# PSUM as eight single-bank tiles instead of two double and four single ones, in a fused linear-attention and token-mixing kernel

## The chip, the cores and the metric

The kernel runs on one core of a Trainium2 chip. The metric is device time in microseconds; smaller is better. A core has five engines that take instructions from queues of their own, each in its written order: TensorE (PE; its weight loads are shown as PEld), VectorE (DVE), ScalarE (ACT), GpSimd (POOL) and SyncE (SP), which here only issues DMA transfers. Matmuls write into PSUM, a memory of eight banks of 512 float32 values in each of 128 partitions; everything else lives in SBUF.

## The reference

```python
def _attn_ref(r, k, v, w, u):            # r, k, v: (4, 8, 768, 48)
    for t in range(S):
        cur = einsum('bhd,bhe->bhde', u[None] * kt, vt)
        y[:, :, t] = einsum('bhd,bhde->bhe', rt, state + cur)
        state = w[None, :, :, None] * state + einsum('bhd,bhe->bhde', kt, vt)

def _moe_ref(x, w_theta, w_tok_r, w_tok_i, w_ch):   # x: y as (4, 768, 384)
    theta = x @ w_theta
    zr, zi = x * cos(theta), x * sin(theta)
    y = einsum('ts,bsd->btd', w_tok_r, zr) + einsum('ts,bsd->btd', w_tok_i, zi)
    u = x + y
    return u + maximum(u @ w_ch, 0.0)
```

A recurrent attention with a per-channel decay `w` and a bonus `u` for the current token gives `x`. Two 768 x 768 matrices then mix the tokens of `x`, rotated by an angle that depends on `x` itself, and a last matrix mixes the channels.

## The kernel before, in words

The tokens of each of the four batches are cut into six chunks of 128, and chunks are taken in pairs: a step `g = 3 * b + pr` is one pair, twelve in all. The recurrence becomes matmuls in chunk form: decayed copies of r and k, scores within a chunk under a triangular mask, and a state handed from chunk to chunk.

`attention(b, pr, base)` makes the tasks of one step. POOL (in the first steps DVE) scales r and k by powers of the decay (`rscale`, L553; `kscale`, L566 and L569), PE transposes them through PSUM (`flips`, L516), and ACT or DVE copies them out (L275, L277). In the first batch (`pj`) the loads hold two neighbouring tokens in one row, and PE puts v back into order (`V`, L600), with a copy `Vev` behind it (L604). `scores` (L614) makes, for each chunk, eight 64-row matmuls, one for each head; even and odd heads go to the two banks of a double tile. `mask` (L619) multiplies the 1024 results by the mask into `mAT`. `PD`, `diag` and `dg` work out the bonus term, and POOL spreads it over v (`yd`, L648). `outer` (L672, L680) and `S` (L690, L700) carry the state. `y` (L712, L717) is one piece for each chunk, both in one double tile; then `x` (L726) adds `yd` for both chunks at once. `x` is transposed, in steps 0 to 5 on PE, from step 6 on by a DMA transpose issued by SP (`turn`, L529). `theta` (L743) multiplies it by `w_theta` for both chunks in one piece, ACT takes the sine (L747) and, in place, the cosine (L750), DVE makes `zr` (L753), POOL `zi` (L756).

`mixing(b, pr, base)` makes, for each chunk of the output, six pieces `mix` of two matmuls (L774), each over one pair of chunks of `zr` or `zi`. They add up in a single bank. `un` (L782) adds x. `un` is transposed (on PE in steps 0 to 3 and 11, otherwise by DMA), `f` (L799) multiplies it by `w_ch` for two chunks, `fin` (L804) is ReLU plus `un`, and SP stores the result (L808). Only the last step does this part chunk by chunk. `token_weights` casts and transposes the two mixing matrices, twelve blocks (`Wcast`, `Wflip` L500, `Wevac`).

The order is written out. `Plan.add` collects each task with its engines, its keys read and written, and the PSUM tiles that it takes (`acq`, with the number of banks) or uses. `ORDER` is a list of (task number, engine, tile numbers ...); `Plan.follow` walks it and emits the tasks in that order, so that each engine's queue has the list's order, and every PSUM tile is the one that the list names. PSUM is cut by

```python
SLOTS = (2, 2, 1, 1, 1, 1)
banks = [ps.tile([C, n, 512], F32, name=f"bank{i}") for i, n in enumerate(SLOTS)]
```

Tasks of two banks (`dbl`: y, theta, f, scores, V) can only take tiles 0 and 1; tasks of one bank may take any. Semaphores between tasks follow from the reads and writes of tiles.

Among the tasks are 108 of the name `warm` (L817), each of two 128 x 128 matmuls on zeros. They compute nothing that is used. The list puts them where PE is to be kept going.

The costs written in the tasks (`dve_op`, `act_op`, `pe_op`, the pairs of SP's loads) were for the search that made the list; when the kernel is built, only the list decides.

Of the kernel before, what the change touches and what calls it, by code (L numbers as in the profile page):

```python
# [22 lines left out]
SLOTS = (2, 2, 1, 1, 1, 1)  # L23
# [4 lines left out]
    (0, 2), (4, 1), (10, 3), (3, 1), (2, 1), (16, 0, 0), (1, 2), (144, 4), (14, 3), (11, 1), (17,  # L28
    0, 3), (7, 2), (13, 3), (145, 4), (32, 0, 4), (8, 3), (33, 0), (18, 2), (34, 0), (12, 3), (9,
    1), (146, 4), (35, 0), (6, 1), (21, 2), (36, 0), (37, 0), (23, 2), (38, 0), (15, 3), (5, 1),  # L30
    (39, 0), (40, 0), (19, 2), (41, 0), (42, 0), (24, 2), (179, 4), (43, 0), (44, 0), (22, 2),
    (45, 0), (150, 1), (46, 0), (47, 0), (20, 2), (48, 0), (49, 0), (50, 0), (153, 2), (51, 0),
    (147, 1), (178, 4), (151, 0, 3), (52, 0), (53, 0), (25, 0, 2), (152, 2), (148, 0, 1), (26, 1),
    (184, 1), (54, 0), (55, 0), (212, 4), (27, 2), (56, 0), (149, 2), (57, 0), (58, 0), (164, 0,
    3), (30, 1), (59, 0), (60, 0), (61, 0), (28, 2), (62, 0), (165, 2), (160, 1), (63, 0), (31,
    3), (158, 0, 1), (140, 4), (154, 0, 0), (181, 1), (64, 0), (65, 0), (155, 2), (161, 0, 2),
    (66, 0), (67, 0), (180, 4), (159, 1), (68, 0), (69, 0), (162, 2), (182, 0, 5), (163, 3), (156,
    0, 0), (183, 2), (70, 0), (71, 0), (157, 1), (185, 0, 2), (213, 4), (72, 0), (73, 0), (74, 0),
    (186, 2), (75, 0), (76, 0), (77, 0), (215, 1), (166, 0), (78, 0), (187, 2), (168, 0, 0), (142,
    4), (79, 0), (194, 1), (169, 0), (216, 0, 2), (141, 2), (170, 1), (268, 4), (80, 0), (195, 0,  # L40
    5), (81, 0), (217, 2), (82, 0), (218, 3), (192, 0, 1), (167, 1), (188, 0, 0), (193, 1), (83,
    0), (196, 2), (270, 4), (84, 0), (189, 2), (198, 0, 5), (143, 2), (171, 0, 3), (197, 3), (190,
    0, 1), (269, 4), (29, 2), (172, 1), (85, 0), (86, 0), (87, 0), (199, 1), (173, 0, 0), (191,
    1), (214, 4), (273, 3), (219, 0, 3), (174, 2), (88, 0), (202, 0, 1), (175, 2), (89, 0), (244,
    4), (90, 0), (203, 0), (276, 3), (91, 0), (92, 0), (220, 2), (200, 0), (204, 1), (252, 4),
    (93, 0), (274, 0, 2), (221, 2), (176, 1), (205, 0, 3), (177, 3), (94, 0), (248, 4), (95, 0),
    (224, 0, 1), (206, 2), (201, 1), (222, 0, 0), (225, 1), (96, 0), (275, 2), (264, 4), (277, 0,
    5), (245, 3), (232, 0, 3), (223, 2), (278, 1), (97, 0), (260, 4), (98, 0), (253, 3), (99, 0),
    (246, 0, 2), (249, 2), (284, 1), (226, 0, 0), (207, 0, 1), (256, 4), (247, 2), (227, 1), (265,
    3), (233, 2), (100, 0), (272, 4), (250, 0, 2), (228, 1), (208, 2), (101, 0), (102, 0), (282,  # L50
    0, 0), (251, 1), (261, 3), (254, 0, 5), (209, 2), (306, 4), (283, 1), (103, 0), (104, 0),
    (229, 0, 2), (266, 0, 3), (230, 2), (255, 2), (105, 0), (262, 0, 2), (231, 3), (271, 4), (210,
    1), (106, 0), (280, 0, 0), (263, 2), (285, 0, 5), (281, 1), (234, 0, 1), (302, 4), (286, 2),
    (267, 2), (307, 3), (107, 0), (235, 0), (415, 0, 2), (257, 2), (211, 3), (236, 1), (330, 4),
    (308, 0, 5), (416, 0), (279, 2), (258, 0, 0), (309, 1), (237, 0, 3), (259, 2), (417, 0), (287,
    3), (331, 4), (238, 1), (288, 0, 1), (403, 0, 5), (289, 2), (418, 0), (404, 0), (314, 4),
    (290, 0), (335, 3), (239, 0, 0), (291, 1), (332, 4), (292, 0, 1), (293, 0), (240, 2), (396, 0,
    3), (303, 3), (294, 1), (322, 4), (405, 0), (241, 2), (406, 0), (243, 3), (397, 0), (242, 1),
    (336, 0, 1), (318, 4), (398, 0), (337, 2), (399, 0), (304, 0, 0), (310, 4), (338, 3), (407,
    0), (305, 2), (400, 0), (401, 0), (364, 4), (419, 0), (402, 1), (295, 0, 1), (323, 3), (408,  # L60
    0), (296, 1), (339, 0, 3), (311, 2), (409, 1), (365, 4), (315, 3), (420, 0), (324, 0, 0),
    (340, 1), (312, 0, 5), (319, 3), (325, 2), (421, 1), (297, 0, 1), (334, 4), (346, 1), (313,
    2), (369, 3), (342, 0, 0), (298, 2), (333, 4), (422, 0, 3), (343, 1), (347, 0, 5), (299, 2),
    (423, 0), (320, 0, 2), (328, 4), (424, 0), (348, 1), (321, 2), (300, 1), (425, 0), (366, 4),
    (410, 0, 0), (316, 0, 5), (341, 3), (411, 2), (344, 0, 1), (317, 1), (426, 0), (454, 4), (329,
    2), (345, 1), (349, 3), (350, 0, 5), (354, 0, 0), (351, 2), (455, 4), (427, 0), (434, 0, 2),
    (372, 3), (352, 0), (370, 0, 1), (353, 1), (326, 4), (355, 0), (371, 2), (428, 1), (441, 0,
    5), (356, 1), (442, 0), (367, 4), (443, 0), (301, 3), (373, 0, 1), (357, 0, 3), (374, 1),
    (486, 4), (435, 0), (358, 2), (436, 0), (380, 1), (461, 3), (378, 0, 0), (327, 2), (444, 0),
    (379, 1), (359, 0, 1), (368, 4), (381, 0, 3), (376, 0, 0), (360, 2), (456, 4), (437, 0), (491,  # L70
    3), (377, 1), (382, 2), (438, 0), (361, 2), (108, 0), (439, 0), (457, 4), (429, 0, 3), (375,
    2), (362, 1), (445, 0), (412, 0, 0), (430, 2), (453, 4), (383, 3), (492, 0, 3), (413, 1),
    (446, 0), (493, 2), (464, 3), (431, 0, 1), (488, 4), (440, 1), (447, 1), (384, 0, 2), (432,
    1), (487, 4), (448, 0, 3), (458, 3), (385, 2), (386, 0, 0), (473, 0, 5), (449, 1), (387, 0),
    (414, 4), (474, 2), (462, 0, 1), (388, 1), (569, 0, 3), (490, 4), (459, 0, 2), (494, 3), (475,
    0), (450, 0, 0), (460, 2), (476, 1), (489, 4), (463, 1), (389, 0, 5), (469, 1), (570, 0),
    (363, 3), (390, 2), (571, 0), (521, 4), (451, 1), (495, 0, 2), (391, 0, 1), (496, 1), (519,
    4), (497, 3), (502, 1), (467, 0, 0), (392, 2), (550, 0, 5), (468, 1), (551, 0), (393, 2),
    (520, 4), (552, 0), (395, 3), (506, 0, 2), (572, 0), (394, 1), (507, 2), (465, 0, 0), (607,
    4), (553, 0), (524, 3), (466, 1), (508, 0), (573, 0), (470, 0, 1), (523, 4), (554, 0), (471,  # L80
    2), (574, 0), (509, 1), (500, 0, 1), (575, 1), (527, 3), (498, 0, 0), (609, 4), (557, 0, 2),
    (501, 1), (558, 0), (525, 0, 3), (522, 4), (559, 0), (499, 1), (472, 3), (503, 0, 1), (555,
    0), (504, 2), (526, 2), (560, 0), (606, 4), (477, 0, 1), (556, 1), (478, 0), (505, 3), (561,
    0), (479, 1), (638, 4), (510, 0, 0), (530, 2), (528, 0, 3), (511, 0), (529, 2), (576, 0, 5),
    (512, 1), (539, 0, 1), (480, 4), (562, 0), (540, 2), (577, 0), (535, 1), (578, 0), (533, 0,
    0), (563, 1), (605, 4), (531, 0, 1), (579, 0), (532, 1), (536, 0, 2), (580, 0), (587, 0, 3),
    (588, 0), (513, 4), (537, 1), (534, 1), (538, 3), (589, 0), (481, 0, 1), (581, 0), (433, 4),
    (613, 3), (482, 2), (541, 0, 0), (582, 1), (542, 0), (483, 2), (640, 4), (594, 0, 2), (543,
    1), (564, 0, 5), (590, 0), (610, 3), (565, 2), (595, 0), (484, 1), (608, 4), (514, 0, 0),
    (544, 4), (566, 0, 1), (515, 2), (485, 3), (516, 2), (596, 0), (567, 1), (614, 0, 5), (671,  # L90
    4), (616, 2), (597, 0), (518, 3), (517, 1), (591, 0), (598, 0), (615, 2), (611, 0, 1), (583,
    4), (599, 0), (612, 2), (643, 3), (592, 0), (545, 0, 0), (593, 1), (600, 1), (639, 4), (619,
    0, 1), (621, 1), (546, 2), (702, 0, 2), (676, 3), (703, 0), (620, 1), (547, 2), (709, 0, 5),
    (452, 4), (622, 0, 3), (704, 0), (623, 2), (548, 1), (710, 0), (601, 4), (549, 3), (705, 0),
    (644, 0, 3), (625, 0, 1), (711, 0), (645, 2), (626, 1), (584, 0, 0), (641, 4), (646, 3), (677,
    0, 3), (568, 4), (627, 0), (712, 0), (678, 2), (628, 1), (706, 0), (624, 3), (713, 0), (585,
    1), (673, 4), (617, 0, 1), (647, 0, 3), (618, 1), (707, 0), (642, 4), (648, 2), (714, 0),
    (602, 0, 0), (708, 1), (672, 4), (654, 1), (652, 0, 1), (603, 1), (727, 0, 2), (728, 0), (674,
# [115 lines left out]
def pe_op(ns):  # L214
    return (ns, 217)
# [27 lines left out]
def build(ctx, tc, nc, r, k, v, w, u, moe_w_theta, moe_w_tok_r, moe_w_tok_i, moe_w_ch, out):  # L243
# [226 lines left out]
    def L2(i):  # L470
        return [("L", i, 0), ("L", i, 1)]
# [397 lines left out]
```

## Time and profile before

| | us |
|---|---|
| median of 6 runs | 141.61 |
| lowest to highest of them | 140.99 to 141.88 |
| the profiled execution, own time | 142.43 |
| its span, first to last instruction | 140.7 |

The granted TensorE clock of the profiled execution is 1.000. The profile shows one execution. "Busy" is the time in which an engine has an instruction under way; a matmul's length holds its fill and drain too, so that the distance from start to start of neighbours (the pitch, below) is shorter than its length. Below, the costliest groups with their counts and mean lengths, from the list of groups by line:

| group | count | mean ns |
|---|---|---|
| PE mix (L774), 128 x 384 | 288 | 326 |
| PE warm (L817), 128 x 128 | 216 | 239 |
| PE scores (L614), 64 rows | 192 | 218 |
| DVE mask (L619), 1024 elements | 24 | 1216 |
| DVE x (L726), 768 elements | 12 | 956 |
| DVE zr (L753), 768 elements | 12 | 950 |
| DVE fin (L804), 768 elements | 11 | 953 |
| DVE un (L782), 384 elements | 24 | 551 |
| ACT sin (L747), 768 elements | 12 | 811 |
| ACT cos (L750), 768 elements | 12 | 876 |
| POOL zi (L756), 768 elements | 12 | 1642 |
| POOL yd (L648), 768 elements | 12 | 1475 |

The mean DMA rate is 196 GB/s; the DMA engines are busy 90% or more of almost every fortieth of the span up to about 65 us, and less so after that.

### The profile page before, as it was taken

To read this page: it belongs to the slowest core of one execution; us is meant where nothing else is said; L and a number is where in the kernel's file an instruction comes from. 1 tells how busy PE (TensorE), PEld (TensorE's weight loads), DVE (VectorE), ACT (ScalarE), POOL (GpSimd) and SP (SyncE) were. 2 spreads that over 40 slices of the span, in tenths; PEclk is the share of its full clock that TensorE was granted. 3 is DMA by queue.
4 is the path that set the end of the run, shared out by engine and by line. 5 is a ranking of instruction groups with operands and counts; after the bars stand their busy time and mean duration, and the time that the engine had idled before them with its cause. 6 is when DMAs were issued, how large, how long until landed. Compare 5 with 4: busy or idle time off the path is not lost.

```text
span 140.7 us, 4021 instructions
## 1 busy us (share of the span) xinstructions
PE 135.7 (96%) x1670; PEld 97.6 (69%) x1670; DVE 100.5 (71%) x144; ACT 76.4 (54%) x119; POOL 85.4 (61%) x78
## 2 busy tenths in 40 slices
PE   6999999999999999999999999999999989999991
PEld 3997878778677676677568676676676645655691
DVE  1379986999457878798998876777989675344720
ACT  3786998999575965855515447855351243300200
POOL 7404379949999999299599099997264044400000
DMA  4999989999999999959997596997969296026660
GB/s 104 270 261 297 276 183 312 387 294 242 301 314 192 181 264 178 206 132 174 226 182 157 106 299 126 230 247 172 168 171 173 56 116 168 0 58 168 224 216 13
DMA packets 72444, 27.59 MB, mean 196 GB/s; under 512 B 67049, under 2 KB 70890, under 8 KB 72426
## 3 DMA queue, kind: packets, MB, share of 16 engines
q1 hardware_dynamic: 72400, 27.34, 85.2%
q8 instruction: 13, 0.21, 0.7%
q14 instruction: 5, 0.04, 0.1%
q10 hardware_dynamic: 26, 0.00, 0.0%
HBM read 20.06 MB, written 4.72 MB: 176 GB/s over the span
## 4 chain that ended last, share of the span: by engine, by line
PE 94%; DVE 2%; issue 1%; ACT 0%; DVEq 0%
PE bank L774 33%; PE bank L516 11%; PE bank L817 11%; PE bank L799 9%; PE bank L743 7%; PE bank L614 5%; PE bank L717 4%; PE bank L672 3%; PE bank L500 3%; PE bank L712 3%; PE bank L641 2%; PE bank L405 1%; PE bank L680 1%; PE bank L402 1%; DVE un L782 1%
## 5 line engine op out<-in xcount | busy, mean ns | idle before, releaser
L774 PE MATMUL bank<-zr,WrT 128*128 128x384 bf16 x144 | 33.4, 326 | 0.0
L774 PE MATMUL bank<-zi,WiT 128*128 128x384 bf16 x144 | 33.1, 326 | 0.0
L619 DVE TENSOR_TENSOR mAT<-bank,mask 128x1024 bf16<-128x1024 f32 x24 | 28.9, 1216 | 1.7 <-PE bank L614 1.6
L756 POOL TENSOR_TENSOR zi<-x,sin 128x768 bf16<-128x768 bf16 x12 | 19.7, 1642 | 10.1 <-ACT sin L747 10.1
L648 POOL TENSOR_TENSOR yd<-dg,vb 128x768 bf16<-128x768 f32 x12 | 17.7, 1475 | 12.9 <-ACT dg L275 5.3
L747 ACT ACTIVATE sin<-bank 128x768 bf16<-128x768 f32 x12 | 9.7, 811 | 19.5 <-PE bank L743 15.8
L817 PE MATMUL bank<-zeros 128*128 128x128 bf16 x216 | 19.3, 239 | 0.0
L569 POOL TENSOR_TENSOR Kw<-ld,wpinv 128x768 bf16<-128x768 f32 x9 | 16.4, 1818 | 3.3 <-DMA ld<-in_k_dram 3.3
L804 DVE SCALAR_TENSOR_TENSOR fin<-bank,un 128x768 f32<-128x768 f32 (+1 forms) x13 | 11.5, 892 | 8.6 <-PE bank L799 8.6
L774 PEld LDWEIGHTS <-WiT 128*128 128x128 bf16 x144 | 12.8, 97 | 6.8
L817 PEld LDWEIGHTS <-zeros 128*128 128x128 bf16 x216 | 15.0, 108 | 2.9 <-issue 2.0
L782 DVE TENSOR_TENSOR un<-bank,x 128x384 bf16<-128x384 f32 x24 | 12.9, 551 | 5.5 <-PE bank L774 5.3
L774 PEld LDWEIGHTS <-WrT 128*128 128x128 bf16 x144 | 12.1, 97 | 6.3
L553 POOL TENSOR_TENSOR Rw<-ld,wpow 128x768 bf16<-128x768 f32 x9 | 16.3, 1819 | 0.0
L275 ACT ACTIVATE RT<-bank 128x1024 bf16<-128x1024 bf16 x12 | 12.3, 1022 | 6.7 <-PE bank L516 6.6
L799 PE MATMUL bank<-Wch,uT 128*128 128x384 bf16 x72 | 13.7, 326 | 0.7 <-DVE un L782 0.6
L726 DVE TENSOR_TENSOR x<-bank,yd 128x768 bf16<-128x768 f32 x12 | 11.5, 956 | 3.9 <-PE bank L717 3.7
L743 PE MATMUL bank<-Wth,xT 128*128 128x384 bf16 x72 | 13.7, 326 | 0.0
L753 DVE TENSOR_TENSOR zr<-bank,x 128x768 bf16<-128x768 f32 x12 | 11.4, 950 | 2.1 <-ACT bank L750 2.1
L799 PEld LDWEIGHTS <-uT 128*128 128x128 bf16 x72 | 6.8, 98 | 5.6 <-DMA uT<-un 0.9
L750 ACT ACTIVATE bank<-bank,pi 128x768 f32<-128x768 f32 x12 | 10.5, 876 | 0.0
L275 ACT ACTIVATE uT<-bank 128x768 bf16<-128x768 bf16 (+1 forms) x5 | 3.3, 684 | 12.1 <-PE bank L516 12.0
(95 smaller groups left out, 221.3 us busy)
## 6 DMA issues: line engine op xcount, KB each, us to landing
ld<-in_r_dram SPq DMA_DIRECT2D x12, 384.0 KB, 5.5
out_dram<-fin SPq DMA_DIRECT2D x11, 384.0 KB, 2.8
ld<-in_k_dram SPq DMA_DIRECT2D x18, 192.0 KB, 5.1
ld<-in_v_dram SPq DMA_DIRECT2D x18, 192.0 KB, 5.3
ld<-in_moe_w_tok_r_dram SPq DMA_DIRECT2D x6, 384.0 KB, 5.2
ld<-in_moe_w_tok_i_dram SPq DMA_DIRECT2D x6, 384.0 KB, 5.7
ld<-in_k_dram SPq DMA_DIRECT2D x3, 384.0 KB, 6.1
ld<-in_v_dram SPq DMA_DIRECT2D x3, 384.0 KB, 5.7
```

Source lines behind the costliest of these rows:

```text
L275: nc.scalar.activation(dst, src, Act.Copy)
L516: nc.tensor.matmul(bank16(tok)[:, i * C:(i + 1) * C], s, ident, is_transpose=True, start=(i == 0), stop=(i == n - 1))
L553: P.add(mul(g, 2.15), lambda e: eng_of[e].tensor_mul(Rw[:, :, :, :D].transpose([0, 2, 1, 3]), Ls[ir].rearrange("p (h n d) -> p h n d", h=H ...
L569: eng_of[e].tensor_mul(Kw[:, :, :, :D].rearrange("p a h d -> p (a h) d"), Ls[ik].rearrange("p (a d) -> p a d", d=D), wpinv.rearrange("p a ...
L619: P.add({DVE: dve_op(8 * C)}, lambda e, tk=tk, c=c: nc.vector.tensor_mul(mAT[:, c].rearrange("p a h t -> p (a h) t"), dbl(tk).rearrange("p ...
L648: P.add({POOL: pool_op(2 * HD, 1.7)}, lambda e: eng_of[e].tensor_mul(yd.rearrange("p a (h d) -> p (a h) d", h=H), wide(dg, D), vb.rearrang ...
L743: nc.tensor.matmul(dbl(th)[:, t, :HD], xT[:, ND * t + dk, :], Wth[:, dk, :], start=(dk == 0), stop=(dk == ND - 1))
L756: P.add({POOL: pool_op(2 * HD, 1.9)}, lambda e: eng_of[e].tensor_mul(zi[:, 2 * pr:2 * pr + 2], x[:, 2 * pr:2 * pr + 2], sn), rd=xk + [("si ...
L774: nc.tensor.matmul(bank(tm)[:, :HD], WT[:, so, to * C:(to + 1) * C], z[:, so], start=(so == 0 and part == 0), stop=(part == 2 * NP - 1 and ...
L782: P.add({DVE: dve_op(HD)}, lambda e, tm=tm, t=t, to=to: nc.vector.tensor_add(un[:, t], bank(tm)[:, :HD], x[:, to]), use=[tm], rd=[("x", zj ...
L799: nc.tensor.matmul(dbl(tf)[:, t - lo, :HD], uT[:, ND * t + dk, :], Wch[:, dk, :], start=(dk == 0), stop=(dk == ND - 1))
L817: nc.tensor.matmul(bank("warm")[:, :C], zeros, zeros, start=True, stop=True, skip_group_check=True)
```

## The change

PSUM becomes eight tiles of one bank. The tasks that held a double tile take single ones: scores and V take two tiles at once, one for each half of the heads and for each chunk; y, theta and f become two tasks, one for each chunk, with one tile each. What reads them is halved with them: two masks of 512 elements for one of 1024, two x, zr, fin, sin, cos and V copies of 384 elements for one of 768. The keys by which tasks wait are cut likewise: y of a chunk waits for its own two masks, un of a chunk for its own x; the transposes, yd and zi still wait for both chunks. `ORDER` is another list, from a new search: all tasks stand in another order, and with other tiles; some copies are on another engine. Three of the costs for the search are changed (in `load` and `turn`), which has no effect on the built program but through the list. There are still 108 warm tasks.

The diff, with the order list and repetitions cut:

```diff
-SLOTS = (2, 2, 1, 1, 1, 1)
+SLOTS = (1, 1, 1, 1, 1, 1, 1, 1)
 ORDER = [
-    (0, 2), (4, 1), (10, 3), (3, 1), (2, 1), (16, 0, 0), (1, 2), (144, 4), (14, 3), (11, 1), (17,
...
+    (0, 2), (4, 1), (13, 3), (2, 1), (3, 1), (16, 0, 7), (1, 2), (146, 4), (14, 3), (17, 0, 5),
...
-        P.add({SP: (ns, 1400)}, lambda e: nc.sync.dma_start(out=dst, in_=src), wr=wr,
+        P.add({SP: (ns, 1700 if nload[0] < 8 else 2300)}, lambda e: nc.sync.dma_start(out=dst, in_=src), wr=wr,
...
-                        nc.tensor.matmul(dbl(tv)[:, c, :HD], spread[q, n, :], vj4[q, :, n, :],
+                        nc.tensor.matmul(bank(tv[c])[:, :HD], spread[q, n, :], vj4[q, :, n, :],
...
-            P.add({ACT: act_op(2 * HD), DVE: dve_op(2 * HD)}, lambda e: copy(
-                e, vb, dbl(tv)[:, :, :HD]), use=[tv], wr=[kv_], prio=pb + 1, name="Vev")
+            for c in range(2):
+                P.add({ACT: act_op(HD), DVE: dve_op(HD)}, lambda e, c=c: copy(
+                    e, vb[:, c], bank(tv[c])[:, :HD]), use=[tv[c]], wr=[kv_ + (c,)],
+                    prio=pb + 1, name="Vev")
...
-            tk = ("A", g, c)
+            tk = [("A", g, c, hi) for hi in range(2)]
...
-                        nc.tensor.matmul(dbl(tk)[:, hi, hp * C:(hp + 1) * C],
+                        nc.tensor.matmul(bank(tk[hi])[:, hp * C:(hp + 1) * C],
...
-            P.add({DVE: dve_op(8 * C)}, lambda e, tk=tk, c=c: nc.vector.tensor_mul(
-                mAT[:, c].rearrange("p a h t -> p (a h) t"),
-                dbl(tk).rearrange("p a (h t) -> p (a h) t", h=HP), bc(mask01, 1, 2 * HP)),
-                use=[tk], rd=["mask"], wr=[kM + (c,)], prio=pb + 3, name="mask")
+            for hi in range(2):
+                P.add({DVE: dve_op(4 * C)}, lambda e, tk=tk[hi], c=c, hi=hi: nc.vector.tensor_mul(
+                    mAT[:, c, hi], bank(tk).rearrange("p (h t) -> p h t", h=HP),
+                    bc(mask01, 1, HP)),
+                    use=[tk[hi]], rd=["mask"], wr=[kM + (c, hi)], prio=pb + 3, name="mask")
...
-        P.add({DVE: dve_op(2 * HD)}, lambda e: nc.vector.tensor_add(
-            x[:, 2 * pr:2 * pr + 2], dbl(ty)[:, :, :HD], yd),
-            use=[ty], rd=[ky], wr=xk, prio=pb + 5, name="x")
+            P.add({DVE: dve_op(HD)}, lambda e, c=c, ty=ty: nc.vector.tensor_add(
+                x[:, 2 * pr + c], bank(ty)[:, :HD], yd[:, c]),
+                use=[ty], rd=[ky], wr=[("x", zj, pr, c)], prio=pb + 5, name="x")
...
-            for t in range(2):
+        for c in range(2):
+            th = ("th", g, c)
+
+            def theta(e, c=c, th=th):
                 for dk in range(ND):
-                    nc.tensor.matmul(dbl(th)[:, t, :HD], xT[:, ND * t + dk, :], Wth[:, dk, :],
+                    nc.tensor.matmul(bank(th)[:, :HD], xT[:, ND * c + dk, :], Wth[:, dk, :],
                                      start=(dk == 0), stop=(dk == ND - 1))
...
-        P.add({DVE: dve_op(2 * HD)}, lambda e: nc.vector.tensor_mul(
-            zr[:, 2 * pr:2 * pr + 2], dbl(th)[:, :, :HD], x[:, 2 * pr:2 * pr + 2]), use=[th],
-            rd=xk, wr=[("zr", zj, pr)], prio=pb + 8, name="zr")
+            P.add({DVE: dve_op(HD)}, lambda e, c=c, th=th: nc.vector.tensor_mul(
+                zr[:, 2 * pr + c], bank(th)[:, :HD], x[:, 2 * pr + c]), use=[th],
+                rd=xk, wr=[("zr", zj, pr, c)], prio=pb + 8, name="zr")
...
-                        nc.tensor.matmul(dbl(tf)[:, t - lo, :HD], uT[:, ND * t + dk, :],
+                        nc.tensor.matmul(bank(tf)[:, :HD], uT[:, ND * t + dk, :],
                                          Wch[:, dk, :], start=(dk == 0), stop=(dk == ND - 1))
...
+                P.add({DVE: dve_op(HD)}, lambda e, t=t, tf=tf: nc.vector.scalar_tensor_tensor(
+                    fin[:, t], bank(tf)[:, :HD], 0.0, un[:, t], op0=Alu.max, op1=Alu.add),
+                    use=[tf], rd=[("un", g % 2, t)], wr=[("fin", g % 2, t)], prio=pb - 98,
+                    name="fin")
```

## The prediction

> **What bounds the kernel now.** First the page: busy time by engine, and the shares of the chain that ended last.
>
> ```profile
> PE 135.7 (96%) x1670; PEld 97.6 (69%) x1670; DVE 100.5 (71%) x144; ACT 76.4 (54%) x119; POOL 85.4 (61%) x78
> ...
> PE 94%; DVE 2%; issue 1%; ACT 0%; DVEq 0%
> ```
>
> TensorE is the bound: 94% of the chain lies on it. But not all of it is work. L817 is filler, matmuls on zeros that the order puts where it expects PE to have nothing to do. Two rows of PE's timeline show it at both ends (start us, length, line, count):
>
> ```profile
> 3.76 4.45 PE L817 MATMUL bank<-zeros 128*128 128x128 bf16 x40
> ...
> 134.36 3.40 PE L817 MATMUL bank<-zeros 128*128 128x128 bf16 x58
> ```
>
> The first 40 stand in 4.3 us (107 ns each), the last 58 in 3.2 us (56 ns each): PE starts at half pace, and a pair costs 0.11 us later on. The last real matmul ends at 134.36. Behind it come fin and the output, 6.4 us, as in any order. So the time is the sum of PE's real pieces, plus filler that stands among them, plus PE's waits. I added the pieces of the before order at the pitch (start to start) that the trace gives each kind: 131.6 us to the end of the real work. The trace has 134.36, so 2.75 us is waiting. Of it 2.1 us can be named, from gaps between PE's starts: 0.71 at 115, 0.36 at 133, 0.30 at 38, 0.30 at 13, 0.24 at 9, 0.15 at 33.
>
> **Two dear things on PE that are neither work nor wait.** In the PE timeline I look at what a scores piece (L614, eight matmuls on 64 of the 128 rows) costs its neighbours:
>
> ```profile
> 71.97 0.49 PE L774 MATMUL bank<-zi,WiT 128*128 128x384 bf16 x2
> 72.39 0.62 PE L614 MATMUL bank<-RT,KT 64*128 64x128 bf16 x16
> 72.94 0.50 PE L774 MATMUL bank<-zr,WrT 128*128 128x384 bf16 x2
> ...
> 96.00 0.81 PE L774 MATMUL bank<-zr,WrT 128*128 128x384 bf16 x4
> 96.74 0.40 PE L614 MATMUL bank<-RT,KT 64*128 64x128 bf16 x8
> 97.07 0.62 PE L516 MATMUL bank<-ident,Kw 128*128 128x128 bf16 x8
> ```
>
> Four L774 take 0.65 elsewhere, here 0.74: entry costs 0.09. Eight L614 then take 0.33, sixteen in a row 0.55. One scores piece inside a run takes 0.23, so leaving costs another 0.10. Each separate excursion to 64 rows costs 0.19 us. The Trainium skill says it too (TensorEngine Tiling, "Key Properties": changing the tiling mode drains TensorE), without a price; the rows give the price.
>
> **The change on PE.** The matmuls are the same 1670 in both programs. I compared the two instruction lists, which hold no times.
> - Scores and V pieces (27, all on 64 rows) stand next to another of them at 6 places before, at 11 after (nine pairs of scores, against three). Five fewer excursions: 5 x 0.19 = -0.95 us. Two one-bank tiles can be had in any two free banks, where scores needed one of two double tiles.
> - Filler pairs ahead of the last real matmul: 79 before, 76 after. 3 x 0.112 = -0.34 us. Filler at the end (29 pairs, now 32) lies under the output.
> - y, theta and f come as two pieces each, with their own waits. PE's pieces of mix also change operands and waits every two matmuls, and hold 0.325 per two (2 x 0.163): a wait that is over costs 0. Upper end, 36 more pieces at 0.03 = 1 us; I take 0, as that row is the same case.
>
> Sum on PE: -1.29 us.
>
> **The waits.** The 0.71 us at 115 shows a queue. The rows are PE's, then SP's:
>
> ```profile
> 114.19 1.14 PE L743 MATMUL bank<-Wth,xT 128*128 128x384 bf16 x6
> 115.88 1.15 PE L799 MATMUL bank<-Wch,uT 128*128 128x384 bf16 x6 [0.55 <-DVE un L782]
> ...
> 104.46 6.89 SPq L529 DMA_TRANSPOSE xT<-x  x2
> 111.46 1.23 SPq L529 DMA_TRANSPOSE uT<-un  x1
> 112.85 2.15 SPq L529 DMA_TRANSPOSE xT<-x  x1
> ```
>
> The view names un, but f(7) needs no new un: its uT transpose stood in SP behind an xT that waited for the x of step 10, was issued at 111.46 instead of about 106, and landed shortly before 115.88. In the new SP list uT(7) follows xT(10), whose x is due at about 102, and f(7) stands 6.9 us behind its last mix; a transpose took 2.8 us from issue to landing (5.5 at worst). The stall goes. The shortest distances between producer and the PE piece that reads a transposed tile are 4.1 to 4.5 us after and 4.6 to 5.3 before, so others have become tighter. I count the waits as equal: 2.75 us in both. From -1.5 (most named ones go) to +3 (below) is what I cannot exclude.
>
> **The other engines.** DVE gets 59 more instructions: 24 masks, 12 x, 12 zr, 11 fin, in halves. Rows of its timeline:
>
> ```profile
> 61.10 1.02 DVE L782 TENSOR_TENSOR un<-bank,x 128x384 bf16<-128x384 f32 x2
> 62.04 0.95 DVE L804 SCALAR_TENSOR_TENSOR fin<-bank,un 128x768 f32<-128x768 f32 x1
> 62.91 0.55 DVE L277 COPY uT<-bank 128x768 bf16<-128x768 bf16 x1
> ...
> 72.97 2.34 DVE L619 TENSOR_TENSOR mAT<-bank,mask 128x1024 bf16<-128x1024 f32 x2
> 75.23 0.55 DVE L782 TENSOR_TENSOR un<-bank,x 128x384 bf16<-128x384 f32 x1
> ```
>
> Two of 384 elements take 0.94, one of 768 takes 0.87: a split costs 0.07. A mask has a pitch of 1.13; its half of 512 elements is in no row, and lies between 0.47 (384) and 0.87 (768). On the line between them it is 0.61, so a split mask costs 0.09. Sum 24 x 0.09 + 35 x 0.07 = 4.6 us. The order also moves some evacuations between DVE and ACT; with them DVE's work at pitch goes from 95.2 to 101.7 us.
>
> Here a rule speaks against the change. The Trainium skill (VectorE: DVE Perf Modes, "The TRN2 errata") has a tensor_tensor take (N+151)/0.96 ns, a fixed 157 ns each, and says to amortize the fixed part over large tiles. By the rule 59 splits cost 9.3 us of DVE, twice the 4.6. The durations agree (2 x 0.55 against 0.956, 0.15 more), but on a busy DVE the next instruction starts 0.08 before the last has ended, and only pitch counts there. I take the row. Whether any of it reaches PE depends on the stage. I laid DVE's pitches against the 10 us stretch of PE's order that releases each: before, the fullest are 60 to 70 (9.6 of 10) and 70 to 80 (8.4). After, 40 to 50 (9.95) and 80 to 90 (9.0). All still fit, so I take 0. By the rule the six splits of 40 to 50 would cost 0.075 more each, 10.4 us in 10: DVE would run over by 0.4, and the gain would be 0.9.
>
> ACT gets 27 more (12 sin, 12 cos, 3 V), each 0.07 (as DVE) to 0.17 (uT: 0.49 for 384 elements, against 0.81): 2 to 4.6 us on an engine 54% busy, 0 on the path. If sin and cos did not hide, zr and zi would be late; the first half now starts half a theta (0.49 us) sooner, which pays for it. POOL loses four casts of 0.8 to ACT and gets three v casts from it.
>
> **Start and loads.** The first loads are now v, k, r for r, k, v; each 384 KB lands 1.5 us after the one before (landing records at 4.6, 6.1, 7.7). V goes first on PE, behind 10 filler pairs instead of 20. Its cast is on POOL (0.82) behind the v load: 5.4, in time for V at 5.9. In the before trace the first k multiply on DVE waited 1.33 us for ACT's wpinvj; in the new ACT order both wpinvj stand one place earlier. I count only the filler, 0 beyond it.
>
> **Sum.** Its own time of the profiled execution is 142.43 (span 140.7), 0.8 over the median of the six runs, 141.61. 142.43 - 1.29 = 141.1 by its account; for the median, **140.3**.
>
> **Rivals.**
> 1. Forecast, the PE sum with equal waits: 140.3, with waits that differ by 0.9 either way 139.4 to 141.2. Chance 0.46.
> 2. The freer banks also remove waits: of the 2.1 us named, those at 115, 38, 13 and 33 (1.46) go and nothing replaces them. 141.61 - 1.29 - 1.46 = 138.9. For it: the room for uT(7). Against: tighter transposes. Chance 0.14.
> 3. The gain goes into small new stalls: PE, a queue in a fixed order, loses 0.02 at each of the 59 more handoffs from DVE, 1.2 us in all: 141.5. Chance 0.14.
> 4. DVE becomes the bound from 40 to 100 us. Its work there at pitch is 47.6 before and 52.2 after, of 60. Before, the busy time by stretches leaves it 12 of these 60 us idle. If that idling is forced by order and handoffs, and only a part can be squeezed out, PE loses what is above 60: with 7.8 left nothing, with 9.1 all of the 1.29. With 10 left it loses 2.2, and the time is 142.5. For it: DVE at 9.95 in one stretch, more instructions in fixed order. Against: in 60 to 70 the old order ran DVE at 9.6 with PE never short. Chance 0.26.
>
> That it does not do what it says is out: the banks and pieces are in the program.
>
> A measurement tells 0.3% (0.42 us) from no change. Faster: 1 and 2, 0.60; the same: 3, 0.14; slower: 4, 0.26. Range 138.8 to 142.7, which takes in most of 4; the forecast's own is 139.4 to 141.2.
>
> **What would show it.** L614 in nine rows of x16, end of PE's real work at 133.0 or so, 6.4 us ahead of the end; masks x48 near 0.69 us; DVE near 106 busy. I am wrong if gaps between PE's starts add up to over 4 us, above all ahead of y and mix where DVE's mask or zr is the last releaser, or if the first 35 us, full of loads, let PE wait.

## The result and the profile after

The changed kernel takes 140.16 us (median of 19 runs, 139.16 to 141.03), beside 141.42 us for the kernel before (38 runs, 140.77 to 141.98, on the same chips). The ratio is 0.991, with a 95% interval of 0.9892 to 0.9928: 1.26 us faster, which was the forecast (140.3). Ratios here and below compare means and leave out the runs of a kernel that lie over 1.5% above its fastest.

The page of the kernel after: busy time by engine, the chain that ended last, and the groups of the halved instructions (count | busy us, mean ns | idle before).

```profile
PE 133.1 (96%) x1670; PEld 96.3 (70%) x1670; DVE 107.6 (78%) x208; ACT 77.2 (56%) x142; POOL 84.9 (61%) x77
...
PE 81%; DMA 10%; DVE 6%; issue 1%; SPq 0%; ACT 0%; DVEq 0%; ACTq 0%
...
L637 DVE TENSOR_TENSOR mAT<-bank,mask 128x512 bf16<-128x512 f32 x48 | 30.9, 681 | 3.8 <-PE bank L631 3.4
...
L767 ACT ACTIVATE bank<-bank,pi 128x384 f32<-128x384 f32 x24 | 13.2, 566 | 0.0
```

DVE has 7.1 us more busy time (100.5 before) and is not the bound. PE is busy 2.6 us less (135.7 before); how much of that is time is worked out below. The chain has less of PE, since it follows three DMA transfers (a first load of k, 4.9 us, an xT and a uT, 4.5 and 4.3 us) and pieces of DVE that the chain of before does not have.

PE's timeline after, at those places (start us, length, line, count, and in brackets the idle time and the releaser that the view names; transposes are L530, scores L631, theta L760, mix L791, f L817, filler L834):

```profile
3.77 2.31 PE L834 MATMUL bank<-zeros 128*128 128x128 bf16 x20
...
11.52 0.61 PE L530 MATMUL bank<-ident,Rw 128*128 128x128 bf16 x8 [0.47 <-DVE Rw L567]
...
19.52 0.61 PE L530 MATMUL bank<-ident,Kw 128*128 128x128 bf16 x8 [0.82 <-DVE x L742]
...
117.18 0.66 PE L817 MATMUL bank<-Wch,uT 128*128 128x384 bf16 x3 [0.63 <-DMA uT<-un]
...
131.51 1.14 PE L817 MATMUL bank<-Wch,uT 128*128 128x384 bf16 x6
132.48 3.74 PE L834 MATMUL bank<-zeros 128*128 128x128 bf16 x64
```

The last real matmul ends at 132.48, against 134.36 before. Added up at the trace's pitches, as the prediction did, PE's order is 129.86 us (131.60 before) and its waits are 2.62 us (2.75 before). So in these two executions the time came out of PE's order and the waits stayed the same in sum; but they are other waits. The four largest are 0.54 at 11, 0.88 at 19, 0.26 at 85, 0.80 at 116 (from start to start; the brackets count from modelled ends and show less). Behind the one at 19 stands a scaling of k on DVE that took 2.54 us (the two other such scalings took 0.94 and 0.96). PE was ready at 18.64. This transpose reads that scaled k, which was done at 18.99; it takes tile 6, which held y of step 0, and the x that reads this y came behind the scaling and was done at 19.47. So somewhat less than half of the wait is for k itself, and the rest for the bank.

The two profiled executions are not alike. After's own time is 140.20, its median; before's was 142.43, 1.0 above its median. Their difference, 2.23, is 1.74 in the order, 0.13 in the waits and 0.37 behind the last real matmul (6.00 against 6.37). The order was to give 1.29; the 0.45 beyond that fits the start, where PE ran at half pace (a filler matmul each 107 ns, later each 56) until about 7.5 us after and 9.2 us before. In the kernel with ACT's halves below, whose start is in the old order, the half pace ended at 7.3 us and PE came to its first outer piece 0.63 us sooner than before. The page's row of the granted clock shows 9 tenths in these slices, so it does not show this slow start. Start and end vary between executions: over the profiles below the half pace ends at 6.7 to 9.2 us, and from the last real matmul to the end it is 4.3 to 6.4 us.

### The profile page after: what moved, and what is told of

It is laid out like the page before. It is cut to its first block, busy times and chain, and to the rows that moved or that the text cites. A ratio compares the mean times of both kernels' runs of the same rounds, so it can differ in the third digit from the quotient of the medians.

```text
span 138.5 us, 4123 instructions
## 1 busy us (share of the span) xinstructions
PE 133.1 (96%) x1670; PEld 96.3 (70%) x1670; DVE 107.6 (78%) x208; ACT 77.2 (56%) x142; POOL 84.9 (61%) x77
## 4 chain that ended last, share of the span: by engine, by line
PE 81%; DMA 10%; DVE 6%; issue 1%; SPq 0%; ACT 0%; DVEq 0%; ACTq 0%
PE bank L791 30%; PE bank L530 10%; PE bank L760 8%; PE bank L817 8%; PE bank L834 7%; PE bank L631 4%; DMA ld<-in_k_dram 4%; PE bank L735 3%; DMA xT<-x 3%; DMA uT<-un 3%; PE bank L514 3%; PE bank L690 3%; PE bank L730 2%; DVE Rw L567 2%; PE bank L659 2%; DVE mAT L637 1%
## 5 line engine op out<-in xcount | busy, mean ns | idle before, releaser
L637 DVE TENSOR_TENSOR mAT<-bank,mask 128x512 bf16<-128x512 f32 x48 | 30.9, 681 | 3.8 <-PE bank L631 3.4
L791 PE MATMUL bank<-zi,WiT 128*128 128x384 bf16 x144 | 33.7, 326 | 0.0
L791 PE MATMUL bank<-zr,WrT 128*128 128x384 bf16 x144 | 33.2, 326 | 0.0
L764 ACT ACTIVATE sin<-bank 128x384 bf16<-128x384 f32 x24 | 11.8, 496 | 14.8 <-PE bank L760 11.9
L567 POOL TENSOR_TENSOR Rw<-ld,wpow 128x768 bf16<-128x768 f32 x10 | 18.2, 1816 | 0.0
L834 PE MATMUL bank<-zeros 128*128 128x128 bf16 x216 | 18.0, 230 | 0.0
L791 PEld LDWEIGHTS <-WiT 128*128 128x128 bf16 x144 | 12.8, 97 | 6.9
L791 PEld LDWEIGHTS <-WrT 128*128 128x128 bf16 x144 | 12.7, 97 | 6.9
L770 DVE TENSOR_TENSOR zr<-bank,x 128x384 bf16<-128x384 f32 x24 | 12.9, 550 | 5.0 <-ACT bank L767 5.0
L821 DVE SCALAR_TENSOR_TENSOR fin<-bank,un 128x384 f32<-128x384 f32 x24 | 12.9, 551 | 4.2 <-PE bank L817 4.1
L834 PEld LDWEIGHTS <-zeros 128*128 128x128 bf16 x216 | 14.1, 103 | 3.0 <-issue 2.0
L817 PE MATMUL bank<-Wch,uT 128*128 128x384 bf16 x72 | 14.8, 326 | 0.6 <-DMA uT<-un 0.6
L760 PE MATMUL bank<-Wth,xT 128*128 128x384 bf16 x72 | 15.3, 326 | 0.1
L742 DVE TENSOR_TENSOR x<-bank,yd 128x384 bf16<-128x384 f32 x24 | 12.9, 551 | 0.8 <-PE bank L735 0.6
L767 ACT ACTIVATE bank<-bank,pi 128x384 f32<-128x384 f32 x24 | 13.2, 566 | 0.0
L289 ACT ACTIVATE Sb<-bank 64x192 bf16<-64x192 f32 x20 | 6.5, 324 | 8.3 <-PE bank L690 8.1
L817 PEld LDWEIGHTS <-uT 128*128 128x128 bf16 x72 | 6.6, 98 | 4.7 <-DMA uT<-un 1.0
```

The lines of the kernel that those rows point to most:

```text
L289: nc.scalar.activation(dst, src, Act.Copy)
L567: P.add(mul(g, 2.15), lambda e: eng_of[e].tensor_mul(Rw[:, :, :, :D].transpose([0, 2, 1, 3]), Ls[ir].rearrange("p (h n d) -> p h n d", h=H ...
L637: P.add({DVE: dve_op(4 * C)}, lambda e, tk=tk[hi], c=c, hi=hi: nc.vector.tensor_mul(mAT[:, c, hi], bank(tk).rearrange("p (h t) -> p h t", ...
L760: nc.tensor.matmul(bank(th)[:, :HD], xT[:, ND * c + dk, :], Wth[:, dk, :], start=(dk == 0), stop=(dk == ND - 1))
L767: P.add({ACT: act_op(HD, True, True)}, lambda e, th=th: nc.scalar.activation(bank(th)[:, :HD], bank(th)[:, :HD], Act.Sin, bias=pi2), use=[th],
L791: nc.tensor.matmul(bank(tm)[:, :HD], WT[:, so, to * C:(to + 1) * C], z[:, so], start=(so == 0 and part == 0), stop=(part == 2 * NP - 1 and ...
```

## The experiments

Each kernel was timed beside the kernel before; ratios are to it.

### Excursions to 64 rows

In the order after, eight pairs of scores pieces were parted by one PE piece, so that there are eight more excursions (the first of eight such moves):

```diff
-    (307, 0, 4, 5), (314, 0, 1), (337, 4),
+    (314, 0, 1), (307, 0, 4, 5), (337, 4),
```

> The new kernel, in which the second scores piece of each of the eight late pairs is put behind the PE piece that followed the pair, so that eight more excursions to 64 rows are made; nothing else moves. PE sum: 8 x 0.19 = 1.5 us more than the new kernel, 141.7, that is the time of before and a little over. If excursions do not matter for the time and the gain came from tiles and order otherwise: within 0.4 us of the new 140.2. If the later second mask matters too: more than 2 us.

Measured: 141.24 us (140.59 to 142.54, 12 runs), ratio 1.0012 [0.9981, 1.0043]. Against after's 0.991 that is 1.0%, 1.4 us with some 0.5 either way, or 0.18 for each excursion. In the trace the same matmuls take 0.21 us longer at each of the eight places, 1.70 in all. One of them, after:

```profile
74.58 0.62 PE L631 MATMUL bank<-RT,KT 64*128 64x128 bf16 x16
75.13 0.50 PE L791 MATMUL bank<-zi,WiT 128*128 128x384 bf16 x2
75.47 0.49 PE L791 MATMUL bank<-zr,WrT 128*128 128x384 bf16 x2
```

and with the pair parted (one line lower in that kernel):

```profile
75.45 0.40 PE L632 MATMUL bank<-RT,KT 64*128 64x128 bf16 x8
75.78 0.50 PE L792 MATMUL bank<-zi,WiT 128*128 128x384 bf16 x2
76.21 0.40 PE L632 MATMUL bank<-RT,KT 64*128 64x128 bf16 x8
76.54 0.50 PE L792 MATMUL bank<-zr,WrT 128*128 128x384 bf16 x2
```

From the first score to the second mix is 0.89 in the one, 1.09 in the other: the same 18 matmuls cost 0.20 more. The five excursions that the change saves are worth 0.9 us by the times and 1.06 by the traces.

### Halves without the new tiles and order

The kernel before, with its double tiles and its order, but mask, x, zr, fin, sin, cos and the V copy each issued as two instructions:

```diff
-        P.add({ACT: act_op(2 * HD)}, lambda e: nc.scalar.activation(
-            sn, dbl(th)[:, :, :HD], Act.Sin), ...
+        P.add({ACT: act_op(2 * HD)}, lambda e: [nc.scalar.activation(
+            sn[:, a], dbl(th)[:, a, :HD], Act.Sin) for a in range(2)], ...
```

> The old order and the old double tiles, but mask, x, zr, fin, sin, cos and the V copy each as two instructions of half the size, one right behind the other, 59 more on DVE and 27 more on ACT. If the halving hides (PE sum): DVE busy rises by some 7 us, PE's real work ends within 0.4 us of the old 134.4, and the time is that of before within 0.3% (141.2 to 141.8). If DVE limits (rival 4): DVE was short of time at 60 to 80 and 100 to 110, so 1 us or more is lost, 142.4 or more, with gaps on PE ahead of y and f.

Measured: 144.36 us (143.58 to 145.08), ratio 1.0201 [1.017, 1.0233]: +2.9 us. Halves alone cost; that they cost nothing needs the rest of the change. So they were taken apart: the same edit on DVE's instructions only, and on ACT's only.

> The old order with the halves on DVE alone (mask, x, zr, fin; 59 more instructions); sin, cos and the V copy whole. Halving all cost 2.9 us. If DVE's load is what the old order could not bear: most of it, 143.5 or above. If the chain through ACT (theta, sin, cos, zr, then the tile is free) was: little, 141.4 to 142.2.

> The old order with the halves on ACT alone (sin, cos, V copy; 27 more instructions); DVE as before. If ACT's chain is the cause of the 2.9 us: 143 or above, since two halves of a cos took 1.14 us where the whole took 0.88, and zr, which sets the tile free for the next PE piece, comes that much later. If DVE's load is: 141.4 to 141.9.

DVE only: 141.13 us (12 runs), ratio 0.9975 [0.9955, 0.9995]: no cost in time. In its trace PE came to theta(10) 0.67 us later than before (114.86 against 114.19) and caught up at f(7), whose transpose landed in 2.8 us there and in 4.4 before (below), so small costs along the way are not excluded. ACT only: 143.40 us (143.33 to 143.68), ratio 1.0137 [1.0112, 1.0163]: +1.9 us. The chain by engine says the same; DVE only, then ACT only:

```profile
PE 95%; DVE 2%; DMA 1%; ACT 0%; issue 0%
```

```profile
PE 68%; ACT 16%; DVE 5%; issue 3%; DMA 3%; POOL 2%; POOLq 0%; ACTq 0%; DVEq 0%
```

The ACT timeline of one step shows what a split costs. Before:

```profile
46.57 0.82 ACT L747 ACTIVATE sin<-bank 128x768 bf16<-128x768 f32 x1
47.26 0.90 ACT L750 ACTIVATE bank<-bank,pi 128x768 f32<-128x768 f32 x1
48.10 0.81 ACT L275 ACTIVATE WrT<-bank 128x768 bf16<-128x768 bf16 x1
```

ACT halved, the same step:

```profile
46.61 0.88 ACT L747 ACTIVATE sin<-bank 128x384 bf16<-128x384 f32 x2
47.52 1.14 ACT L750 ACTIVATE bank<-bank,pi 128x384 f32<-128x384 f32 x2
48.59 0.80 ACT L275 ACTIVATE WrT<-bank 128x768 bf16<-128x768 bf16 x1
```

From the sine to what stands behind the cosine it is 1.53 us before and 1.98 in halves: 0.45 a step, 0.22 a split. In the trace the halves do not overlap here: each cosine half waits for a semaphore that ACT itself sets at its instruction before. In the kernel after, where each half has a tile of its own, they overlap by some 0.1 us:

```profile
49.11 0.48 ACT L764 ACTIVATE sin<-bank 128x384 bf16<-128x384 f32 x1
49.48 1.03 ACT L767 ACTIVATE bank<-bank,pi 128x384 f32<-128x384 f32 x2
50.41 0.83 ACT L289 ACTIVATE WrT<-bank 128x768 bf16<-128x768 bf16 x1
```

The second sine takes 0.37 us and the two cosines 0.93 from start to start, so that two of each are some 1.67 us, against 1.53 whole: 0.07 a split. That the tiles make the difference fits these waits; no run has tiles of its own with the old order. In the old order zr waits for both cosines, and PE's next scores wait for the double tile that zr frees. PE's timeline of the ACT-halved kernel:

```profile
49.71 0.40 PE L614 MATMUL bank<-RT,KT 64*128 64x128 bf16 x8 [0.28 <-DVE zr L753]
```

Like this one (0.35 from start to start), two more waits at 72 and 123 us have zr behind them, 0.25 and 0.42; one of 0.47 at 61 has a copy of uT on ACT. They are most of the 1.9. After the change no wait of PE above 0.2 us has zr or a cosine behind it. DVE's and ACT's halves together cost 1.3 us more than their sum (2.9 against 1.9 and -0.35). In the profiles 1.07 of this stands ahead of f(7), where PE waited 0.87 us in the kernel with all halves, 0.49 with ACT's, 0.02 with DVE's and 0.71 before; there the landing of one transpose decides (below), so it need not be a cost of the splits.

### Smaller pieces still

After, with each mask as two of 256 elements: 48 more DVE instructions.

```diff
-                    mAT[:, c, hi], bank(tk).rearrange("p (h t) -> p h t", h=HP), bc(mask01, 1, HP)),
+                    mAT[:, c, hi, q:q + 2], bank(tk).rearrange(...)[:, q:q + 2],
+                    bc(mask01, 1, 2)) for q in (0, 2)],
```

> The new kernel with each mask as two instructions of 256 elements, 48 more on DVE at about 0.08 us each by the rows of the halved kinds, 3.9 us of DVE work. If DVE still hides: within 0.4 us of the new 140.2. If the new order has used up DVE's room (40 to 50 us was 9.95 of 10): 1 us or more, 141.2 or above, with gaps on PE ahead of y.

Measured: 141.13 us (139.58 to 141.93, 12 runs), ratio 0.9956 [0.9923, 0.9988]; against after 0.46%, +0.65 us with an interval of about 0.5 either way, for 48 more splits (DVE's busy time grows by 2.7 us, to 110.3). DVE is close to the bound only in one stretch. The busy times from 20 to 30 us (PE, PEld, DVE, ACT, POOL; clock, DMA share, GB/s), after:

```profile
20.00:30.00 10.00, 10.00 (x187) 8.45 (x185) 10.00 (x20) 9.38 (x18) 7.01 (x6) 1.00 0.91 248
```

with quarters:

```profile
20.00:30.00 10.00, 9.71 (x175) 8.09 (x175) 10.00 (x27) 8.27 (x18) 6.40 (x5) 1.00 0.93 260
```

There DVE is full in both, and with quarters PE no longer is.

### The wait at 115 in the order before

The prediction put the 0.71 us before f(7) down to SP's order. Test: in the order before, SP issues uT(7) ahead of xT(10).

```diff
-    (665, 4), (694, 0), ..., (747, 0), (734, 4),
+    (694, 0), ..., (747, 0), (734, 4), (665, 4),
```

> The kernel before with SP's transpose uT of step 7 put ahead of xT of step 10, so that it is issued when its un is done (about 110.6) instead of at 111.46. If the 0.71 us wait of PE at 115 came from SP's order, as the prediction had it: it goes, 140.7. If un itself, late on DVE behind three masks, set it: the transpose is issued at 110.6 at the earliest and 0.0 to 0.5 us is saved, 140.9 to 141.4.

Measured: 142.46 us (9 runs), ratio 1.0069 [1.0039, 1.0099]: 1.0 us slower. SP's timeline in that kernel:

```profile
104.37 2.03 SPq L530 DMA_TRANSPOSE xT<-x  x1
110.54 1.21 SPq L530 DMA_TRANSPOSE uT<-un  x1
111.81 3.26 SPq L530 DMA_TRANSPOSE xT<-x  x2
```

uT(7) still could not be issued before 110.5, and xT(10) now stood behind it; theta(10) on PE then waited 1.47 us for it (3.9 us from its issue to its landing). One cause is one engine further back, in DVE's timeline of before:

```profile
105.66 3.48 DVE L619 TENSOR_TENSOR mAT<-bank,mask 128x1024 bf16<-128x1024 f32 x3
109.16 0.96 DVE L726 TENSOR_TENSOR x<-bank,yd 128x768 bf16<-128x768 f32 x1
110.03 0.55 DVE L782 TENSOR_TENSOR un<-bank,x 128x384 bf16<-128x384 f32 x1
```

The un that uT(7) transposes stood behind three masks and an x, though its last mix had ended at 106.6. So the next run moved this un ahead of one mask and the x, and uT(7) ahead of xT(10) as before:

```diff
-    (684, 1), ..., (693, 0, 0), (726, 1), (665, 4), ..., (734, 4),
+    (726, 1), (684, 1), ..., (693, 0, 0), (734, 4), (665, 4), ...,
```

> The kernel before with the un of step 7 (mix of chunk 2, batch 2) put one mask and one x earlier in DVE's order, and the DMA transpose uT of step 7 ahead of xT of step 10 on SP. If DVE's order was the cause of PE's wait at 115 (un done at 110.5 in before), un is done about 2 us earlier, the transpose lands ahead of f, and some 0.7 us is saved, 140.7. If the two transposes disturb each other on the way as they did with SP's order alone: 142 or more.

Measured: 141.15 us (12 runs), ratio 0.9973 [0.9953, 0.9992]: 0.38 us faster, half of what was expected. DVE's and then PE's timeline of that kernel:

```profile
105.84 2.36 DVE L620 TENSOR_TENSOR mAT<-bank,mask 128x1024 bf16<-128x1024 f32 x2
108.11 0.55 DVE L783 TENSOR_TENSOR un<-bank,x 128x384 bf16<-128x384 f32 x1
```

```profile
103.31 0.62 PE L517 MATMUL bank<-ident,Kw 128*128 128x128 bf16 x8 [0.24 <-POOL Kw L570]
...
114.36 1.14 PE L744 MATMUL bank<-Wth,xT 128*128 128x384 bf16 x6
115.34 1.14 PE L800 MATMUL bank<-Wch,uT 128*128 128x384 bf16 x6
```

The wait at 115 is gone (f starts 0.98 after theta, its pitch); 0.35 us appears at 103, ahead of both edits, in this one profile. But three things made the wait in the execution of before. The un came 3.4 us after its last mix. SP's order held the transpose back for another 0.9 (111.46 for 110.54). And the transpose took long to land. From issue to landing of uT(7), in us, before and then with DVE's halves only, where un and the transposes stand in the order of before:

```profile
uT<-un SPq DMA_TRANSPOSE x1, 4.4
```

```profile
uT<-un SPq DMA_TRANSPOSE x1, 2.8
```

With DVE's halves it was issued later still, at 112.20, and f(7) did not wait. Before, f(7) was due at 115.17; with a landing in 2.8 us the transpose would have been there at 114.2. So by these times the wait would not have been there with any one of the three gone. The edit moved un and its transpose together, so the part of DVE's order alone is not shown; nor is why it gained only half, though executions with a quick landing would have had nothing to gain.

### The wait at 116 in the order after

After has a like wait, 0.80 us before f(8). SP's timeline of after:

```profile
112.80 1.22 SPq L543 DMA_TRANSPOSE uT<-un  x1
114.64 1.91 SPq L543 DMA_TRANSPOSE xT<-x  x1
```

From the issue of uT(8) to the f that reads it is 4.4 us, where 2.8 was usual. The chain of after has this transfer with its landing:

```profile
112.80 4.33 DMA uT<-un
```

In the last kernel below the same transpose landed in 2.7 us, though the next one was issued 1.7 us behind it, so this wait too hangs on one slow landing. The edit moves the first piece of f(8) three mix pieces later, with its fin, and exchanges the tiles of two theta pieces:

```diff
-    (856, 0, 1), (837, 1), (883, 0), (857, 1), (863, 0), (840, 4), (870, 0), (796, 0, 1),
+    (837, 1), (883, 0), (863, 0), (840, 4), (870, 0), (856, 0, 1), (857, 1), (796, 0, 0),
...
-    (792, 0, 0),
+    (792, 0, 1),
```

> The new kernel with the first f piece of step 8, which waited 0.8 us for its DMA-transposed input at 116.4, put three mix pieces (0.98 us) later, its fin with it, and the two theta pieces of step 11 with their tiles exchanged. If that wait is on the path to the end: 0.8 us less than the new kernel, 139.4. If it only moves (theta of step 11 or a later f waits instead): within 0.3 us of 140.2.

Measured: 139.18 us (138.96 to 140.54, 5 runs), ratio 0.985 [0.9798, 0.9903]: 0.6% below after's, some 0.85 us with 0.8 either way, just clear of noise. PE's timeline there has no wait left:

```profile
115.13 1.14 PE L792 MATMUL bank<-zi,WiT 128*128 128x384 bf16 x6
116.11 0.65 PE L818 MATMUL bank<-Wch,uT 128*128 128x384 bf16 x3
116.60 1.14 PE L792 MATMUL bank<-zr,WrT 128*128 128x384 bf16 x6
```

### Filler

The prediction counted a filler pair among PE's work at 0.11 us. Here 60 pairs emit nothing, in the order after and (57 pairs) in that before:

```diff
-                for _ in range(2):
+                for _ in range(0 if 16 <= i < 76 else 2):
```

> The new kernel without the filler pairs 16 to 75 (the 60 pairs that stand among the real work after the first 8 us; the first 16 and the last 32 stay). If filler is real time on PE: up to 60 x 0.11 = 6.7 us less. If filler stands where PE would wait for loads or other engines in any case: within 0.5 us of the new 140.2, with the same time as gaps on PE in the first 35 us. A slower PE clock through the gaps would show in the granted clock and in warm pairs of 0.21 us.

> The kernel before without the filler pairs 22 to 78 (57 pairs). As for the new one: within 0.5 us of before (141.4) if filler only fills, up to 6 us less if it costs. What matters for the prediction is whether the two differ by the same amount: if the new order's gain of 0.34 us from three fewer pairs is real, the gap between new and old grows or shrinks by about that when both lose their filler.

After without them: 139.18 us (138.58 to 140.05), ratio 0.9847 [0.981, 0.9885]: 0.9 us less than after with some 0.6 either way, for 6.7 us of filler (60 x 0.112). The rest, 5.8 us, came back as waits and as clock. The page's row of the granted clock (tenths, 40 slices of 3.4 us):

```profile
PEclk9999995599999999999999999999999999999999
```

In two slices (20.6 to 27.5 us) the clock was halved, after gaps of 1.41 and 0.92 us that the filler closes in the order after. From 20.7 to 29.9 us PE fell 2.8 us further behind its order, most of it in matmuls at half pace. In the order before, the times spread from 139.0 to 143.54 us (median 141.41, 12 runs), and they follow the mean granted clock of each run: 142.9 to 143.5 at 0.952, 141.0 to 142.2 at 0.963 or 0.964, 141.43 at 0.976, 139.0 and 139.5 at 0.988, 139.61 at 1.0. The ratio, 0.9878 [0.984, 0.9916], rests on the four fastest runs alone (139.0 to 141.02); by its median this kernel is as fast as before. The Trainium skill (TensorE: Matmul & The Clock Gate, Part 1, "What's actually happening") describes a gate that halves PE's clock after an idle window, which it puts at about 3.4 us; the row agrees in the half, its 5, but here the single gaps ahead of it were of 1.41 and 0.92 us.

### Together

The moved f(8) without the filler pairs 16 to 75:

> The new kernel with the f piece of step 8 put later and without the 60 filler pairs inside. Alone they gave 0.85 and 0.9 us by their ratios. If they add up: 138.4. If the late filler-free start and the later f meet the same limit: 139.2, as each alone.

Measured: 139.11 us (138.2 to 139.32), ratio 0.9821 [0.9789, 0.9852]: between what each gives alone (0.985) and the two added up (0.979), and by its median no better than either. Whether what the one frees the other had in part already is not shown; the clock is 0.975 or 0.987 in all six runs.

Last, only the filler pairs from 46 on dropped, f(8) moved, and the first piece of theta(7), which waited for its transpose at 85 us, put behind the next y piece:

```diff
-    (575, 0, 3), (657, 4), (543, 3), ..., (608, 0, 1),
+    (657, 4), (543, 3), ..., (608, 0, 1), (575, 0, 3),
...
-                for _ in range(2):
+                for _ in range(0 if 46 <= i < 76 else 2):
```

> The new kernel with the f piece of step 8 put later, the first theta piece of step 7 put behind the y piece that followed it (it waited 0.26 us), and without the filler pairs 46 to 75 only, so that the filler of the first 18 us still keeps PE going. Late waits gone: 0.8 + 0.26; filler after the wait for k of step 2: up to 0.8. Together 138.3 to 138.7 if these are all on the path; above 139 if the loads set the pace up to 35 us whatever PE does.

Measured: 137.65 us (135.83 to 138.34, 6 runs) beside 141.61, ratio 0.9677 [0.9625, 0.973]. It beats both kernels, by 3.2% the one before and by some 2.3% the one after; the ratio rests on four of the six runs, and by the medians it is 2.8% and 1.8%. So a few edits to the list by hand gained more than the change itself did. Its runs go with the clock too: 135.83 and 137.54 at 1.0, 137.6 and 137.7 at 0.987, 138.25 and 138.34 at 0.975. What is left in PE's timeline of the execution at 0.975:

```profile
19.16 0.61 PE L531 MATMUL bank<-ident,Kw 128*128 128x128 bf16 x8 [0.81 <-DVE x L743]
...
21.29 0.48 PE L699 MATMUL bank<-Sb,ident 128*128 128x384 bf16 x1 [0.92 <-DVE Sb L719]
...
26.73 1.14 PE L761 MATMUL bank<-Wth,xT 128*128 128x384 bf16 x3
```

Two waits on DVE, where it is full, and behind them three theta matmuls in 0.93 us (start to start) where 0.49 is the full pace.

## Why the prediction was right, and where it was not

- **The sum on PE, -1.29 us: right.** The measured medians differ by 1.26. The rows stand as said: nine scores rows of sixteen, masks at 681 ns for 690, DVE 107.6 busy for 106. The end of PE's real work is 132.48 for "133.0 or so"; as shown above, the start of the execution of before, from which that was reckoned, was a slow one.
- **Excursions, 5 x 0.19: right,** by a run of their own: 0.18 each by the times, 0.21 by the traces. They are some 0.9 to 1.06 of the 1.26.
- **Filler, 3 x 0.112: the price holds only where PE has nothing to wait for.** Of 6.7 us of filler, 0.9 was time. Whether the three pairs gave their 0.34 is open.
- **Waits equal: right in the sum, by replacement and partly by luck.** It holds for two executions, one profile of each kernel, and the landing of a single transpose moves a wait by up to 1.6 us. "The stall goes" was right for the place, but its cause was only a part of it: "its uT transpose stood in SP behind an xT", "issued at 111.46 instead of about 106". The step that failed is the reading of SP's queue as the cause. SP could not have issued it before 110.5, as the un was late on DVE; and it landed 4.4 us after its issue, not 2.8, which the prediction's own times show (111.46 to shortly before 115.88). Moved ahead on SP, f(7) did lose its wait, and theta(10) got one of 1.47. In place of this wait came f(8) with 0.80. The prediction had warned of transposes with less room (4.1 to 4.5 us); this one took 4.3.
- **DVE's halves at 0: right.** By the old order with them alone (-0.35 us, no cost in time). The forecast that 40 to 50 us would be DVE's fullest stretch (9.95) was wrong: it was busy 8.20 there, and full from 20 to 30. Rival 4 does not hold for this change, but 48 splits more cost 0.65.
- **ACT's halves at 0: right, and so was the price.** "Each 0.07 to 0.17" is 0.07 in the kernel after; it is 0.22 where the halves share a double tile. The cover is not ACT's idle half alone, as "ACT 54% busy" suggests: in the old order, with the same idle half, they cost 1.9 us. That what pays is what the sum named last, that the first half starts sooner, here in a tile of its own and in an order laid out for it, is argued.
- **The rivals.** Rival 2 did not come: single banks took away no waits in sum, and part of the wait at 19 us is for a bank. Rival 3 did not come either: the four largest waits leave 0.14 us for all others, so there are no small new stalls at the 59 handoffs.

The halves in the old order take 144.36 us, the change 140.16: by the two ratios (1.0201 and 0.991) tiles and order together are worth about 4.1 us, of which the halves that they need eat 2.9. That takes the parts as adding up, and the 2.9 is measured in the old order alone. How much of that is the tiles and how much the search stays open. The old order cannot use single tiles, and the new order with double tiles was not tried.

## What to carry to other kernels

When an engine is full and its order is written out, add up its pieces start to start and look for what costs between kinds of pieces; here eight-matmul pieces on 64 rows cost about 0.2 us each time that they stand alone, and five fewer of them were most of the gain. Splitting instructions to free a resource sooner is not free in itself: here the halves on whole tiles cost 2.9 us, those on DVE none of it alone and those on ACT 1.9, and they paid only together with split tiles and an order for them. When a view names the last releaser of a wait, make sure that it is what the waiting piece needs. Here the un that it named for f(7) was a later one; the piece needed a transposed tile. Then go back through the landing, the issue and the producer of that tile, each with its time, before blaming the queue that stands nearest.

## What the hardware showed that was not expected

- A sine or cosine from PSUM split from 768 into 2 x 384 elements cost ACT 0.22 us where both halves work in one double tile, and 0.07 where each has its own; the like split on DVE costs 0.07 to 0.09.
- Filler on PE is two things: 60 pairs were worth only 0.9 of their 6.7 us, yet without them PE's clock was halved for about 7 us, and in the order before, the times of one kernel spread by 4.5 us with the granted clock.
- The end of PE's slow start (6.7 to 9.2 us) and the stretch from the last matmul to the end (4.3 to 6.4 us) differ between executions, so that one profiled execution can stand 1.0 us from its kernel's median.
- The same DMA transpose takes 2.7 to 2.8 us from its issue to its landing in one kernel and 3.8 to 4.5 in the next. Another transpose behind it does not explain it: with one issued 1.3 to 1.7 us behind, it landed in 2.7 to 2.8 us three times. The cause stays open.
